# Attention over memory slots, then a three-way maxout layer, on one core: k and q of batch 0 load first, GpSimd packs k, v and ones for batches 2 to 7, and batch 0 divides its softmax by a ones product

## The chip, the cores and the metric

The kernel runs on one core of a Trainium2 chip. Its time is the device time of one execution in microseconds (us). The core has five engines with instruction queues of their own: TensorE (PE, matmuls; PEld is its weight load), VectorE (DVE), ScalarE (ACT), GpSimd (POOL) and SyncE (SP). Each engine works its queue off in order, and waits at an instruction whose inputs are not there. Loads that change the type from fp32 to bf16 are issued by GpSimd; they stand in its queue beside its other instructions.

## The reference

There are 8 batches, 8 heads, 576 positions, heads of width 64 and 32 memory slots.

```python
a = softmax(phi, axis=2)                        # (b, h, s, m)
k_m = einsum('bhsm,bhsd->bhmd', a, k)
v_m = einsum('bhsm,bhsd->bhmd', a, v)
attn = softmax(q @ k_m^T / sqrt(64), axis=-1)   # over the 32 slots
x = (attn @ v_m), heads side by side            # (4608, 512)
h = maximum(maximum(x @ w1, x @ w2), x @ w3)    # w1, w2, w3: 512 x 768
out = h @ w_out                                 # 768 x 512
```

## The kernel before

Two heads share the 128 partitions as a pair; there are NP = 4 pairs, and NC = 9 positions per partition. The kernel does not compute x. It multiplies v_m into the weights first (`fold`), so that the 32 slots of 4 heads (128 rows, two groups g) are the contraction of all large matmuls. It also uses max(a, b, c) = max(a - c, b - c) + c with w3 as c: `w_diff` takes w3 off w1 and w2 in place (for batch 0 the fold adds a second term instead, because w_diff comes later), and w3 @ w_out is made once.

The whole order of work is a list written out by hand. An item is a letter, a part and a batch (`F8@0` is part 8 of F in batch 0). The items are issued in this order, and each engine gets its share of them in this order. A "!" moves the copy out of PSUM from VectorE to ScalarE or back. The items are:

- L0, L1, L2, L3: load phi, k, v, q of a batch. H0 to H3: halves of k and v of batch 0. Y0 to Y3: w1, w2, w3, w_out. All go through GpSimd (lines 90 to 115), but for phi of batch 0, which goes through SP (line 88).
- I: the identity for transposes, made by GpSimd.
- Z: matmuls on zeros that keep TensorE at work early on (line 128). Z38 is 38 of them.
- E: exp of phi on ScalarE (line 196). B: 72 small matmuls that sum e times k, v and a constant 1 over the positions (line 209), 192 columns each; batch 1 does it in two parts, k and ones (128 columns), and v (64). kvo is the tile with k, v and ones; there are two, one for even and one for odd batches.
- N: reciprocal of the sums and the division on VectorE (lines 225 to 239). K: transpose of the result on TensorE and its copy kvt (line 254).
- Q: two VectorE transposes of q (line 269). S: scores on TensorE and their exp e2 on ScalarE (lines 291, 300).
- a, s, c, m, X: the softmax over the 32 slots on VectorE, once for each group g: a transposes 32 x 32 blocks (line 310), s sums (line 318), c takes the reciprocal (line 327), m multiplies (line 332), X transposes back into attn (line 340).
- W: w3 transposed, O: w3 @ w_out (lines 153, 161), once, with copies w3o on ScalarE. V: w_diff (line 182).
- D0, D1, D2, D4: the fold of v_m into w1 and w2, to wp (line 363); D3 into w3o, to wp3.
- F: 12 parts per batch, four matmuls each (line 389). Even parts end in a relu to h, odd parts in the max with h, which is hT (line 402).
- T: output rows, 128 at a time: six matmuls of hT with w_out (line 420), two of attn with wp3 (line 429), a copy to ot and a store on SP (line 450).

PSUM has four buffers of two banks, taken in turn by all items that use TensorE. kvo, the phi and the q tiles are there twice, so a load of batch b waits until batch b - 2 is through with its tile. A load through GpSimd also waits for the one eight places before it in the queue, since eight semaphores are used in turn.

Of the kernel before, what the change touches and what calls it, by code (L numbers as in the profile page):

```python
# [15 lines left out]
def kernel(  # L16
# [47 lines left out]
    for i in range(2):  # L64
        kvo = const.tile([P, 3, NP, NC, D], BF16, name=f"kvo{i}")
        kvos.append(kvo)
    w_sb = const.tile([P, NP, 3, DF], BF16, name="w_sb")
    w3T = const.tile([P, FT, NP, P], BF16, name="w3T")
# [6 lines left out]
    def by_pair(src, b):  # L75
        return src[b].rearrange("h s d -> (h s) d").rearrange(
            "(j p c) d -> p j (c d)", p=P, c=NC
        )

    halves = [slice(0, NP // 2), slice(NP // 2, NP)]  # L80

# [10 lines left out]
    def load_kv(b, i, h=slice(0, NP)):  # L92
        kv = loaded.setdefault(b, {})["kv"] = kvos[b % 2]
        nc.gpsimd.dma_start(  # L94
            out=kv[:, i, h].rearrange("p j c d -> p j (c d)"),
            in_=by_pair((k, v)[i], b)[:, h],
        )

# [21 lines left out]
    nc.vector.memset(warm, 0.0)  # L120
    nc.vector.memset(kvos[0][:, 2], 1.0)
    nc.vector.memset(kvos[1][:, 2], 1.0)

# [53 lines left out]
    def w_diff(n):  # L177

        c, end = n * BANK, (n + 1) * BANK
        while c < end:  # L180
# [7 lines left out]
            c = e  # L188

    st = {}  # L190

# [6 lines left out]
    def att_kv(b, part=None):  # L198
# [4 lines left out]
        cols = {None: slice(0, 3), 0: slice(0, 3, 2), 1: slice(1, 2)}[part]  # L203
        nd = {None: 3 * D, 0: 2 * D, 1: D}[part]
        for c in range(NC):
            for j in range(NP):
                for a in range(NG):
                    r = slice(HP * a, HP * (a + 1))
                    nc.tensor.matmul(  # L209
                        kvp[M * j : M * (j + 1), a, 0:nd],  # L210
                        lhsT=s["e"][r, j, c, :],
                        rhs=kv[r, cols, j, c, :],
                        start=(c == 0),
                        stop=(c == NC - 1),
                        tile_position=(HP * a, M * j),
                    )
# [59 lines left out]
    def att_score(b):  # L276
# [22 lines left out]
        for a in range(NG):  # L299
# [4 lines left out]
                scale=0.125,  # L304
            )

    def att_t(b, g):
# [176 lines left out]
    def issue(b, n, swap):  # L484

        i = int(n[1:]) if len(n) > 1 else None
        {
            "I": lambda: make_identity(nc, ident),
            "Y": lambda: load_w(i) if i < 3 else load_wo(),
            "L": lambda: load_ph(b) if i == 0 else load_q(b) if i == 3 else load_kv(b, i - 1),  # L490
            "H": lambda: load_kv(b, i % 2, halves[i // 2]),
            "E": lambda: [att_exp(b, h) for h in (halves if b == 0 else [slice(0, NP)])],
            "B": lambda: att_kv(b, i),
# [7 lines left out]
            "m": lambda: att_mul(b, i),  # L501
            "X": lambda: att_back(b, i),
            "D": lambda: fold(b, i, swap),
# [9 lines left out]
    for w in """  # L513
        H3@0 I@0 H2@0 H0@0 H1@0 E@0 Z38@0 B@0 N@0 Z3@0 K@0 L3@0 Q0@0 Q1@0 Z7@0 S@0 a0@0 Y2@0
        Y3@0 a1@0 s0@0 s1@0 c1@0 Z6@0 W0@0 W2@0 Y0@0 Y1@0 W1@0 Z10@0 O1@0 O0@0 O2@0 m1@0 D1@0!
        c0@0 m0@0 X0@0 D0@0 O3@0 L0@1 L1@1 L3@1 L2@1 X1@0 F8@0 F0@0 V0@0 F2@0 D4@0! D2@0 L0@2
        V2@0 F10@0 F6@0 F11@0 F9@0 E@1 F4@0 F3@0 F1@0 F7@0 F5@0 D3@0 B0@1 T3@0 N0@1 Q0@1 K0@1!
        T1@0 Q1@1 S@1 V1@0 E@2 L1@2 B1@1 L0@3 N1@1 a0@1 a1@1 K1@1 T2@0! s0@1 s1@1 D0@1 c0@1
        D2@1 c1@1 m0@1 D1@1! m1@1 T0@0! L2@2 X0@1 X1@1 F4@1! F5@1 L3@2 L2@3 F10@1 L1@3 F11@1
        F8@1 F0@1 F2@1 F3@1 L3@3 F6@1 F9@1 F1@1 E@3 F7@1 B@2 D3@1 N@2 Q1@2 Q0@2 T3@1 K@2! T2@1!  # L520
        S@2 a0@2 T1@1 T0@1! L0@4 D0@2 s0@2 L2@4 D1@2! a1@2 c0@2 m0@2 s1@2 c1@2 m1@2 X1@2 T4@1!
        X0@2 D3@2 L1@4 B@3 L0@5 N@3 D2@2 F6@2! Q1@3 F10@2 F2@2 F8@2 Q0@3 K@3! F3@2 F0@2 F7@2
        S@3 F1@2 F11@2 F4@2 F9@2 F5@2 E@4 D0@3 L1@5 a1@3 a0@3 D1@3! T0@2! T1@2 s0@3 D3@3 s1@3
        c1@3 m1@3 X1@3 D2@3 B@4 c0@3 E@5 T2@2! L2@5 L3@5 m0@3 X0@3 L3@4 F2@3 N@4 F0@3 F8@3
        F10@3 F1@3 F6@3 F3@3 K@4 F4@3 F7@3 F9@3 F5@3 D0@4 B@5 N@5 D1@4! F11@3 T3@2 Q0@5 K@5
        T4@3! Q1@5 S@5 L0@6 Q0@4 Q1@4 a1@5 a0@5 T1@3 s1@5 D0@5 S@4 T0@3! L0@7 s0@5 c0@5 a0@4
        c1@5 m0@5 D3@5 a1@4 m1@5 D1@5! D2@5 E@6 s1@4 X1@5 c1@4 T2@3! X0@5 s0@4 L2@7 T3@3 m1@4
        L1@7 F4@5 F0@5 F2@5 L3@7 c0@4 X1@4 m0@4 F1@5 F5@5 F3@5 X0@4 E@7 F10@5 F8@5 F9@5 D3@4
        B@7 N@7 D2@4 F11@5 F6@5 F4@4 F10@4 F8@4 Q0@7 L3@6 Q1@7 K@7 F7@5 L1@6 F0@4 Q1@6 S@7 a1@7
        L2@6 F11@4 s1@7 F5@4 a0@7 T1@5 s0@7 F6@4 c1@7 T3@5 c0@7 m0@7 F2@4 F1@4 F3@4 D1@7! D3@7  # L530
        B@6 m1@7 N@6 D2@7 T2@5! X1@7 Q0@6 K@6 F9@4 F7@4 S@6 T4@5! D0@7 a0@6 s0@6 X0@7 D0@6 a1@6
        s1@6 c1@6 m1@6 X1@6 T3@4 D3@6 D2@6 c0@6 D1@6! T0@5! T1@4 F6@7 F2@7 F0@7 m0@6 X0@6 F3@7
        F4@6 F8@6 F7@7 F9@6 F6@6 F2@6 F1@7 F5@6 F4@7 F5@7 F0@6 F7@6 F10@6 F8@7 F10@7 F9@7 F1@6
        F11@7 T2@4! F11@6 T2@7! F3@6 T1@7 T0@7! T2@6! T0@6! T3@6 T1@6 T0@4! T4@7! T3@7
    """.split():
        n, b = w.rstrip("!").split("@")
        issue(int(b), n, w.endswith("!"))
# [30 lines left out]
```

## Time and profile before

| | before |
|---|---|
| median of 5 runs | 167.4 us (166.72 to 167.59) |
| the profiled execution | 167.4 us |
| its span | 165.6 us |
| PE busy | 156.2 us (94%) |
| DVE busy | 104.6 us (63%) |
| ACT busy | 98.7 us (60%) |
| POOL busy | 28.3 us (17%) |
| moved by DMA | 31.77 MB, mean 192 GB/s |

The span runs from the first to the last instruction in the profile; the rest of the time lies around it. A matmul's end is modelled, and matmuls overlap, so the durations of single matmuls add up to more than the time they take. The chain of waits is the better guide: it lists, in order of time, the pieces of work that the end hung on. A GpSimd instruction that issues a load takes about 0.75 us there; the data arrive later.

### The profile page before, as it was taken

The page shows a single profiled execution, that of the slowest core. Times are in us where ns is not written, and L with a number is a line of the kernel's source. Part 1 is how long each engine was busy: PE and PEld are TensorE (multiplying, and loading weights), DVE is VectorE, ACT ScalarE, POOL GpSimd, SP SyncE. Part 2 cuts the span into 40 slices and gives each one's busy share as a digit, 9 for nine tenths or more (in the row PEclk, how much of TensorE's full clock was granted, in tenths as well). Part 3 has the DMA queues.
Part 4 walks back from the last instruction along what each step waited for, and adds up shares of the span by engine and source line. Part 5 has one row for each costly group of instructions (what it writes and reads, how often), then busy time and mean ns, then how long its engine had stood idle before and what let it go on. Part 6 is the DMA issues. An engine that isn't in the chain of part 4 may idle for free.

```text
span 165.6 us, 4664 instructions
## 1 busy us (share of the span) xinstructions
PE 156.2 (94%) x2006; PEld 87.6 (53%) x2024; DVE 104.6 (63%) x196; ACT 98.7 (60%) x148; POOL 28.3 (17%) x43
## 2 busy tenths in 40 slices
PE   7998799999799999999999999999999999999990
PEld 2444444674357544755674447765544678544450
DVE  5406782497686756999399798979999066610010
ACT  4200206964598458997954799993859867124320
POOL 7952110050510500710104600000000000000000
PEclk9999999999999999999999999999999999999999
DMA  5999999999999999999999999993113200024332
GB/s 151 149 204 213 205 211 225 263 208 279 311 242 257 204 243 326 259 280 213 261 238 340 233 261 235 261 205 100 69 67 123 105 32 0 35 99 183 129 150 107
DMA packets 21973, 31.77 MB, mean 192 GB/s; under 512 B 1216, under 2 KB 16576, under 8 KB 21952
## 3 DMA queue, kind: packets, MB, share of 16 engines
q0 software_dynamic: 16080, 21.43, 67.4%
q1 hardware_dynamic: 5728, 9.90, 16.9%
q8 instruction: 16, 0.26, 0.6%
q10 hardware_dynamic: 144, 0.13, 0.2%
q14 instruction: 5, 0.04, 0.1%
HBM read 39.32 MB, written 9.44 MB: 294 GB/s over the span
## 4 chain that ended last, share of the span: by engine, by line
PE 82%; DMA 10%; POOL 3%; issue 2%; ACT 0%; DVE 0%; POOLq 0%; ACTq 0%
PE acc L389 29%; PE po L420 28%; DMA wo_sb<-in_moe_w_out_dram 10%; PE po L429 8%; PE wps L363 6%; PE kvp L209 4%; PE po L161 3%; POOL kvo L94 2%; PE sc L291 2%; PE po L438 1%; PE po L461 1%; PE kvtp L254 1%; POOL qq L102 0%; POOL w_sb L108 0%; PE po L469 0%
## 5 line engine op out<-in xcount | busy, mean ns | idle before, releaser
L420 PE MATMUL po<-wo_sb,hT 128*128 128x512 bf16 x195 | 50.4, 380 | 0.8
L389 PE MATMUL acc<-attn,wp 128*128 128x288 bf16 x384 | 50.2, 286 | 0.0
L402 DVE TENSOR_TENSOR hT<-acc,h 128x576 bf16<-128x576 f32 x48 | 34.4, 752 | 15.6 <-PE acc L389 10.1
L389 PEld LDWEIGHTS <-wp 128*128 128x128 bf16 x384 | 36.8, 98 | 12.4 <-issue 1.7
L141 ACT COPY ot<-po 128x512 f32<-128x512 f32 x35 | 20.6, 592 | 30.0 <-PE po L429 24.1
L141 ACT CAST wp<-wps 128x1024 bf16<-128x1024 f32 (+1 forms) x32 | 30.4, 1003 | 4.2 <-PE wps L363 4.1
L420 PEld LDWEIGHTS <-hT 128*128 128x128 bf16 x210 | 19.2, 98 | 23.5 <-issue 3.9
L139 ACT ACTIVATE h<-acc 128x576 bf16<-128x576 f32 x46 | 27.6, 664 | 4.4 <-PE acc L389 4.0
L429 PE MATMUL po<-wp,attn 128*128 128x512 bf16 x62 | 18.4, 379 | 0.0
L128 PE MATMUL po<-warm 128*128 128x512 bf16 x62 | 16.6, 425 | 1.4 <-DVE warm L120 1.2
L332 DVE TENSOR_TENSOR t<-t,sm 128x576 bf16<-128x576 bf16 x16 | 11.8, 746 | 0.3
L128 PEld LDWEIGHTS <-warm 128*128 128x128 bf16 x64 | 6.5, 106 | 9.7 <-issue 3.3
L318 DVE TENSOR_REDUCE sm<-t 128x18 f32<-128x576 bf16 x16 | 11.5, 738 | 0.2
L269 DVE STREAM_TRANSPOSE qT<-qq 128x576 f32<-128x576 f32 x16 | 11.5, 753 | 0.0
L300 ACT ACTIVATE e<-sc 128x576 bf16<-128x576 f32 x16 | 9.6, 655 | 2.9 <-PE sc L291 2.9
L310 DVE STREAM_TRANSPOSE t<-e 128x288 f32<-128x288 f32 x16 | 7.2, 464 | 6.3 <-ACT e L300 6.2
L94 POOL DMA_DIRECT2D kvo<-in_v_dram x9 | 6.8, 755 | 23.2 <-PE wps L363 14.3
L196 ACT ACTIVATE e<-ph 128x1152 bf16<-128x1152 f32 (+1 forms) x9 | 9.7, 1072 | 1.7 <-DMA ph<-in_phi_dram 1.6
L429 PEld LDWEIGHTS <-attn 128*128 128x128 bf16 x62 | 6.1, 98 | 7.3
L90 POOL DMA_DIRECT2D ph<-in_phi_dram x7 | 5.3, 763 | 25.2 <-ACT e L196 16.8
L478 DVE COPY ot<-po 128x256 f32<-128x256 f32 x1 | 0.4, 424 | 14.2 <-PE po L469 14.2
L209 PE MATMUL kvp<-kvo,e 64*32 64x192 bf16 (+2 forms) x648 | 8.3, 235 | 1.0 <-issue 0.9
(48 smaller groups left out, 108.6 us busy)
## 6 DMA issues: line engine op xcount, KB each, us to landing
out_dram<-ot SPq DMA_DIRECT2D x35, 256.0 KB, 5.5
qq<-in_q_dram POOLq DMA_DIRECT2D x8, 576.0 KB, 18.8
ph<-in_phi_dram POOLq DMA_DIRECT2D x7, 576.0 KB, 19.3
kvo<-in_k_dram POOLq DMA_DIRECT2D x7, 576.0 KB, 18.6
kvo<-in_v_dram POOLq DMA_DIRECT2D x7, 576.0 KB, 15.8
w_sb<-in_moe_w_dram POOLq DMA_DIRECT2D x3, 768.0 KB, 19.6
wo_sb<-in_moe_w_out_dram POOLq DMA_DIRECT2D x1, 768.0 KB, 16.7
ph<-in_phi_dram SPq DMA_DIRECT2D x2, 288.0 KB, 3.0
```

The costliest lines, as they stand in the source:

```text
L94: nc.gpsimd.dma_start(out=kv[:, i, h].rearrange("p j c d -> p j (c d)"), in_=by_pair((k, v)[i], b)[:, h],)
L128: nc.tensor.matmul(po[:, 0:BANK], lhsT=warm[:, 0:P], rhs=warm, start=True, stop=True)
L139: nc.scalar.activation(out=out_, in_=in_, func=AF.Relu)
L141: nc.scalar.copy(out=out_, in_=in_)
L209: nc.tensor.matmul(kvp[M * j : M * (j + 1), a, 0:nd], lhsT=s["e"][r, j, c, :], rhs=kv[r, cols, j, c, :], start=(c == 0), stop=(c == NC - 1 ...
L269: nc.vector.transpose(out=s["qT"][:, j].rearrange("p j c r e -> p (j c r e)").bitcast(FP32), in_=loaded[b]["q"][:, j].rearrange("p j c d - ...
L318: nc.vector.tensor_reduce(out=sm, in_=s["t", g].rearrange("p n r e -> p n e r"), op=ALU.add, axis=mybir.AxisListType.X,)
L332: nc.vector.tensor_tensor(out=t, in0=t, in1=s["sm", g].unsqueeze(2).to_broadcast([P, S // HP, R, 2]), op=ALU.mult,)
L389: nc.tensor.matmul(acc[:, h, 0:SH], lhsT=wps[b][:, g, w * DF + ft * P : w * DF + (ft + 1) * P], rhs=attn[:, g, c0 : c0 + SH], start=(g == ...
L402: nc.vector.tensor_tensor(out=hT[:, ft, (b % 2) * S : (b % 2 + 1) * S].rearrange("p (h n) -> p h n", h=2), in0=a, in1=s["h1", ft], op=ALU.max,
L420: nc.tensor.matmul(po, lhsT=hT[:, fc, c0 : c0 + P], rhs=wo_sb[:, fc, :], start=(n == 0), stop=False,)
L429: nc.tensor.matmul(po, lhsT=attn[:, g, c0 : c0 + P], rhs=wp3s[b][:, g, :], start=False, stop=(g == NG - 1),)
```

## The change

The change has four parts.

1. Batch 0's loads: GpSimd first makes the identity and sets two small columns of ones, then loads k in two halves, q, w3, w_out, v in two halves, w1, w2. Before it loaded half of v, then made the identity, then k, the rest of v, q, w3, w_out, w1, w2. The k/v sums of batch 0 are split in two, as those of batch 1 already were.
2. For batches 2 to 7, GpSimd copies k and v from kvo into a tile kvr, where each position has 64 of k, 64 of v and a one. The sums then use 129 columns instead of 192.
3. For batch 0 the softmax over slots is divided by another way: a matmul with a block matrix of ones gives the sums, ScalarE takes exp(-ln) of them, and VectorE multiplies e2 by it into attn. Items M, R and X replace a, s, c, m and X there.
4. The written order is new throughout; the warm-up matmuls are 45 instead of 64.

```diff
+    kvrs = [
+        const.tile([P, NP, NC, 2 * D + 2], BF16, name=f"kvr{i}") for i in range(2)
+    ]
...
+    FULL = 2
...
+    def pack(b, i):
+        nc.gpsimd.tensor_copy(
+            out=kvrs[b % 2][:, :, :, D * i : D * (i + 1)], in_=kvos[b % 2][:, i]
+        )
...
+    blkones = const.tile([P, P], BF16, name="blkones")
+    nc.vector.memset(blkones, 0.0)
+    for i in range(P // M):
+        nc.vector.memset(blkones[M * i : M * (i + 1), M * i : M * (i + 1)], 1.0)
...
+    ln = const.tile([P, S], FP32, name="ln")
+    ONES = {(0, 0), (0, 1)}
...
-        nd = {None: 3 * D, 0: 2 * D, 1: D}[part]
+        nd = {None: 3 * D if b < FULL else 2 * D + 1, 0: 2 * D, 1: D}[part]
+        kvr = kvrs[b % 2]
...
-                        rhs=kv[r, cols, j, c, :],
+                        rhs=kv[r, cols, j, c, :]
+                        if b < FULL
+                        else kvr[r, j, c, 0:nd],
...
+    def ones_sum(b, g):
+        s = st[b]
+        e2 = s["e2"]
+        sm = acc_pool.tile([P, 2, BANK], FP32, name="sm", tag="acc")
+        for h in range(2):
+            nc.tensor.matmul(
+                sm[:, h, 0:SH],
+                lhsT=blkones,
+                rhs=e2[:, g, h * SH : (h + 1) * SH],
+                start=True,
+                stop=True,
+            )
+        s["sm", g] = sm
+
+    def ones_rec(b, g):
+        s = st[b]
+        sm = s["sm", g]
+        nc.scalar.activation(
+            out=ln.rearrange("p (h n) -> p h n", h=2),
+            in_=sm[:, :, 0:SH],
+            func=AF.Ln,
+        )
+        r = work.tile([P, S], FP32, name="r")
+        nc.scalar.activation(out=r, in_=ln, func=AF.Exp, scale=-1.0)
+        s["r", g] = r
+
+    def ones_mul(b, g):
+        s = st[b]
+        nc.vector.tensor_tensor(
+            out=attns[b // 2][:, g, (b % 2) * S : (b % 2 + 1) * S],
+            in0=s["e2"][:, g, 0:S],
+            in1=s["r", g],
+            op=ALU.mult,
+        )
...
-            "I": lambda: make_identity(nc, ident),
+            "I": lambda: [make_identity(nc, ident)]
+            + [nc.gpsimd.memset(x[:, :, :, 2 * D : 2 * D + 1], 1.0) for x in kvrs],
...
+            "r": lambda: pack(b, i),
...
-            "X": lambda: att_back(b, i),
+            "X": lambda: (ones_mul if (b, i) in ONES else att_back)(b, i),
+            "M": lambda: ones_sum(b, i),
+            "R": lambda: ones_rec(b, i),
...
-        H3@0 I@0 H2@0 H0@0 H1@0 E@0 Z38@0 B@0 N@0 Z3@0 K@0 L3@0 Q0@0 Q1@0 Z7@0 S@0 a0@0 Y2@0
-        Y3@0 a1@0 s0@0 s1@0 c1@0 Z6@0 W0@0 W2@0 Y0@0 Y1@0 W1@0 Z10@0 O1@0 O0@0 O2@0 m1@0 D1@0!
-        c0@0 m0@0 X0@0 D0@0 O3@0 L0@1 L1@1 L3@1 L2@1 X1@0 F8@0 F0@0 V0@0 F2@0 D4@0! D2@0 L0@2
...
+        E@0 I@0 H0@0 H2@0 Z25@0 B0@0 N0@0 L3@0 Z2@0 K0@0! Y2@0 Q0@0 Q1@0 Y3@0 H1@0 Z9@0 S@0
+        Z2@0 M0@0 R0@0 W1@0 X0@0 H3@0 W0@0 W2@0 M1@0 R1@0 Y0@0 Y1@0 Z7@0 O1@0 L0@1 O0@0 O2@0
+        L1@1 X1@0 L3@1 B1@0 N1@0 O3@0 K1@0 L2@1 L2@2 D3@0 L1@2 L0@2 D1@0 D0@0! F6@0 F8@0 V0@0
+        F2@0 F10@0 F0@0! D4@0 D2@0 F4@0 V1@0 F11@0 L3@2 F7@0 F5@0 F9@0 F3@0 F1@0 E@1 B0@1 N0@1
+        Q1@1 Q0@1 T1@0 K0@1! T3@0 r1@2 S@1 B1@1 V2@0 L0@3 L1@3 a0@1 s0@1 a1@1 N1@1 r0@2 s1@1
+        T2@0! K1@1 D2@1 c0@1 m0@1 L2@3 L3@3 c1@1 L1@4 L2@4 X0@1 m1@1 D1@1! X1@1 D0@1 T0@0! F8@1
...
+        N@4 D3@3 T3@2 Q0@4 K@4 F2@3 F0@3 F4@3 L0@6 Q1@4 L1@6 F3@3 L2@6 S@4 F1@3 F5@3 a0@4 L3@6
+        F10@3 F11@3 F8@3 F9@3 F6@3 s0@4 F7@3 D1@4! D2@4! E@5 r1@5 T2@3! a1@4 D3@4 L2@7 r0@5
+        D0@4 B@5 c0@4 m0@4 N@5 s1@4 T3@3 Q0@5 E@6 K@5 Q1@5 c1@4 T4@3! S@5 m1@4 T0@3! X1@4 X0@4
```

The items of the new order that the diff names r0 and r1 are the copies of k and of v for a batch.

## The prediction

> **What bounds the kernel now.** I read first the chain of waits in order of time (columns: start us, us, what). It shows what the end hangs on.
>
> ```profile
> 6.21 16.66 DMA wo_sb<-in_moe_w_out_dram
> 22.88 0.14 issue
> 23.02 3.40 PE po L161 x15
> ...
> 30.71 0.77 PE wps L363 x32
> 31.48 4.52 PE acc L389 x36
> ...
> 36.33 0.64 PE kvp L209 x72
> ...
> 41.24 0.88 issue
> ...
> 42.80 0.30 DVE kvn L229
> ...
> 47.71 5.90 PE acc L389 x48
> ...
> 77.57 0.74 PE kvp L209 x72
> ```
>
> Up to 22.9 us the end hangs on the arrival of w_out, the seventh load in GpSimd's queue. From 23.02 us to 161.56 us it is TensorE, one matmul after another. The only gaps that stand out are 0.88 and 0.30 us in batch 1; after 47.71 us there is hardly any. So there are two ways to win: start this stretch earlier, or take matmul time out of it. Everything else can only put gaps into it.
>
> Next the timeline of GpSimd, to see when loads land. From the tenth on, each load waits for the load eight places before it; the bracket is that wait.
>
> ```profile
> 9.28 0.75 POOL L90 DMA_DIRECT2D ph<-in_phi_dram  x1 [0.67 <-DMA kvo<-in_k_dram]
> 10.72 0.74 POOL L94 DMA_DIRECT2D kvo<-in_k_dram  x1 [0.69 <-DMA kvo<-in_k_dram]
> 12.16 0.74 POOL L102 DMA_DIRECT2D qq<-in_q_dram  x1 [0.70 <-DMA kvo<-in_v_dram]
> 15.00 0.74 POOL L94 DMA_DIRECT2D kvo<-in_v_dram  x1 [2.10 <-DMA qq<-in_q_dram]
> 19.63 0.75 POOL L90 DMA_DIRECT2D ph<-in_phi_dram  x1 [3.89 <-DMA w_sb<-in_moe_w_dram]
> ```
>
> Half a k or v lands every 1.44 us, a whole q takes 2.84, a weight about 4: a stream with no holes, in issue order. Last VectorE's timeline in batch 1, and the page's row of the same operation:
>
> ```profile
> 43.01 0.83 DVE L310 STREAM_TRANSPOSE t<-e 128x288 f32<-128x288 f32 x2
> 45.17 0.39 DVE L327 RECIPROCAL sm<-sm 128x18 f32<-128x18 f32 x2
> 45.48 1.42 DVE L332 TENSOR_TENSOR t<-t,sm 128x576 bf16<-128x576 bf16 x2
> 46.81 0.83 DVE L340 STREAM_TRANSPOSE attn<-t 128x288 f32<-128x288 f32 x2
> ```
> ```profile
> L332 DVE TENSOR_TENSOR t<-t,sm 128x576 bf16<-128x576 bf16 x16 | 11.8, 746 | 0.3
> ```
>
> The softmax chain ends at 47.64 us and the first matmul that needs it starts at 47.71. In batch 1 VectorE is just in time: anything that holds it there is paid by TensorE.
>
> **What the Trainium skill says.** "SBUF — State Buffer", section "Who interferes with whom": a VectorE instruction with two SBUF inputs contends with a GpSimd instruction that reads SBUF, and the later one blocks until the first is through. Here that is L332 (t and sm both in SBUF) against the new packing; the max of L402 and the other copies have one operand in PSUM. No GpSimd instruction of the trace reads an SBUF tile beside L332, so the trace neither confirms nor denies it. "GPSIMD Engine Reference", section "Elementwise — side-by-side cycle accounting": between 1.03 and 1.8 cycles per element at 1.2 GHz, by the loop. "ScalarE: Activation LUTs", section "Table sets: the hidden batching unit": ln and exp share a set, so the new Ln loads no table; the trace has one table load, of this set.
>
> **The change, part by part** (item names as in the written order; b1 is batch 1).
>
> *Order of loads.* v of batch 0 (two halves, 2 x 1.44 = 2.88 us of the stream) moves from before q to behind w_out. So q, w3 and w_out land 2.88 us earlier; w1, w2 and all behind them keep the same bytes ahead. But GpSimd now makes the identity (0.6 us from 2.06 to 2.66) and two small memsets (about 0.1 each, as the L552 memsets) before its first load, which is issued near 2.2 instead of 1.25 us. The stream loses between 0 (phi from SP's queue fills the engines until 4 us anyhow) and 1.0 us; I take 0.5. So w3_o starts at 23.02 - 2.88 + 0.5 = 20.64.
>
> *What the start can use.* From there TensorE runs, in the new order: O x4 at 1.30 (six matmuls of 512 columns; such sixes take 1.29 in the chain) = 5.20; the v half of batch 0's k/v sums, now apart, 72 matmuls of 64 columns, about 0.85 (the same for b1: 0.18 + 0.67); a wait of 0.7 for ScalarE's copy of the last O (0.59) less the small transpose beside it; D3 0.35; D1, D0 at 0.77; a wait of 0.24 for D1's copy (0.96 on VectorE); five F at 0.49 (48 matmuls in 5.90). D4 starts at 20.64 + 5.20 + 0.85 + 0.7 + 0.35 + 1.54 + 0.24 + 2.45 = 31.97, when w2 (used at 30.6 before, so there by 31.1) has landed. Before, D4 started at 30.71: 1.26 later. In exchange two F (0.98) and D3 (0.35) are done by then: 1.33. The 2.9 us won at the door are spent on the split sums and on two copies that TensorE now waits for: -0.07.
>
> *Ones product for batch 0.* Per half, two transposes, sum, reciprocal and product leave VectorE (0.46 + 0.74 + 0.25 + 0.75 + 0.46 = 2.66, 5.3 in all) and one product stays (0.75). Added: four matmuls of 288 columns (0.5) and Ln and Exp twice on ScalarE (4 x 0.66, as L300). All fall between the scores at about 15 us and 20.6 us; ScalarE idles 6.54 us there before its first copy of w3o. Cost 0; without that cover attn of batch 0 would be 2.6 us late, and it is not needed before 29. Fewer warm-up matmuls: 0 as well, they fill waits.
>
> *Narrower k/v sums.* Batches 2 to 7 go from 192 to 129 columns. The chain has 0.74 for 192 and 0.64 for 128: 0.10 x 6 = -0.6. Ends: 0 if weight loads set the pace (72 loads span 0.9 us at either width), and -1.4 if columns do (nine rounds of eight tiles, 63 columns at 0.42 ns each, x6).
>
> *Packing.* Twelve copies of 2304 elements on GpSimd: an estimate from the page above, 2.0 to 3.5 us each; I take 2.7, 32 us in all beside 28.3 us now busy. Each waits for its load, and behind it in GpSimd's queue stand loads: behind v of b2, phi and k of b3 (issued at 34.79 and 43.8 before, now near 48). The stream still has k, phi and q of b2 to move by then, so it doesn't run dry. The copies free kvo early, which lets k and v of b4 on go out sooner.
>
> *Batch 1.* In the new order nothing makes VectorE wait before b1's first transpose (the 2.25 us wait for kvn goes), so the gaps of 0.88 and 0.30 should go: -1.18. But from the end of the scores to the first F TensorE has 5.3 us of work (B1 0.74, K 0.1, T 1.72 twice, three D 1.0), and VectorE needs 0.75 for the exp and 5.4 for its items (0.83 + 1.40 + 0.39 + 1.42 + 0.83 + 0.29 + 0.19): a wait of 0.85.
>
> Sum without contention: -0.07 - 0.6 - 1.18 + 0.85 = -1.0. New gaps that a new order brings after 47.7 us, where there were none: I allow +0.7 (one copy late per two batches). That is 167.1 us.
>
> *Contention.* v of b2 is five loads behind w2: 31.1 + 1.6 + 4 x 2.88, and some 1.2 for output rows, gives 45 us; its packing runs 45 to 47.7. The scores of b1 end near 41.7; L332 is due 0.75 + 2.9 later, at 45.35, and its second at 46.7. Whichever comes first, one product stands behind a packing: 1.6 to 2.9 us, less if the packing is 2.0 us; I take 1.9, straight into TensorE's wait, as batch 1 has no slack. In b2 (6.6 us of TensorE work between scores and first F against 5.9 on VectorE) and b5 (6.5) half of such a hit shows: +0.3 in all. Batches 3, 4, 6, 7 have 9 us or more. +2.2 together. Bounds: 0 (no such hold) to +5 (both products hit in b1, b2, b5).
>
> The profiled execution took 167.4 us, 1.8 outside its span of 165.6; it is also the median shown, so nothing is to be shifted: 167.4 - 0.3 + 2.2 = 169.3.
>
> **Rivals.** *(a) Contention, 0.48:* the forecast, 169.3, own range 167.6 to 171. *(b) No hold, and the start comes out even, 0.24:* 167.1. For it: L332 is slow already (746 ns for 576 elements), so the shared interface may have room. *(c) The other side, faster, 0.16:* no hold, the first load loses nothing (-0.5) and the sums run at column rate (-0.8 more): 165.8. It decides from the start of w3_o: at 20.2 us or earlier with L332 still at 0.75 us, the gain stands. Against it: both copies that TensorE waits for are real. *(d) GpSimd late, 0.12:* between the last q transpose of b4, which frees the tile for q of b6, and the sums of b5, TensorE has 7.7 us of work; in that time GpSimd must do pack, load, pack. At 3.5 us a pack that is 7.75. Each microsecond above costs two there and about one each in b3 and b4: at 4.5 us, 171.5. That w_out doesn't come earlier would be a fifth; nothing speaks for it, as loads land in issue order.
>
> **How the numbers follow.** The measurement tells 0.3% (0.5 us) from no change. Faster: all of (c), a third of (b), little of (a): 0.16 + 0.08 + 0.03 = 0.27. Same: 0.14 of (b), 0.04 of (a): 0.18. Slower: the rest, 0.55. The range reaches from (c) at 165.8 to (d) at 171.6; signs are mixed, so (a)'s own range stands above.
>
> **What would show it.** w3_o starting near 20.6 us; D4 near 32; TensorE idle before the last w3o-dependent D3. Sums of batches 2 to 7 at 0.64 in the chain. Packing rows of 2.0 to 3.5 us. In b1 an L332 well over 0.75 us, or an idle before it ended by GpSimd, and TensorE waiting 2 to 3 us before its first L389 row of b1. If L332 stays at 0.75 us beside a running packing, (a) falls. If packings wait on one another with TensorE idle before the sums, it was (d).

## The result and the profile after

The changed kernel takes 168.34 us (median of 22 runs, 167.6 to 169.58), the kernel before 167.24 us (43 runs, 166.23 to 167.96). The ratio is 1.0071, with a 95% interval of 1.0056 to 1.0086: slower by 1.1 us between the medians. The profiled execution of the changed kernel is the slowest of the 22, 169.58 us with a span of 167.8 us; so its stages are read one by one below, and its end is not compared with the median. The ratios in this document leave out executions more than 1.5% above the fastest of their kernel: five of the twelve of the kernel packed in pieces and three of the six of the one whose packings nobody reads.

| | before | after |
|---|---|---|
| PE busy | 156.2 us | 154.6 us |
| DVE busy | 104.6 us | 106.9 us |
| POOL busy | 28.3 us | 53.7 us |
| first matmul of w3 @ w_out | 23.02 us | 21.09 us |
| accumulation of batch 1 in the chain | 47.71 us | 49.58 us |
| accumulation of batch 2 in the chain | 66.21 us | 67.81 us |

The gain at the door (the earlier start of w3 @ w_out, called w3_o below), 1.93 us, is gone by batch 1. The chain of waits of the changed kernel (start us, us, what) shows where. Line numbers have moved: L332 is now L385 (the product of the softmax), L389 is L442 (accumulation), L363 is L416 (fold), L209 is L225 (k/v sums), L340 is L393 (transpose back into attn); L104 is the packing.

```profile
8.70 23.81 DMA w_sb<-in_moe_w_dram
...
32.55 0.84 PE wps L416 x32
33.40 0.60 PE acc L442 x4
...
45.67 0.76 DVE t L385
46.95 2.07 DVE t L385
49.58 5.79 PE acc L442 x46
...
62.99 2.02 DVE t L385
65.43 0.76 DVE sm L371
66.52 0.76 DVE t L385
67.81 2.14 PE acc L442 x16
70.29 0.65 PE kvp L225 x70
```

Before, this stretch was TensorE with two small gaps. Now VectorE's softmax stands in it in batches 1 and 2, and one product in each batch takes 2.0 us instead of 0.75. The k/v sums are at 0.65 us, down from 0.74 (in batch 2 at 0.73, down from 0.87). TensorE's own timeline shows what it waits for in batch 1 (the bracket is the wait, and what ended it): two of the 48 matmuls need only the first half of attn, the others wait for the second half.

```profile
48.03 0.41 PE L442 MATMUL acc<-attn,wp 128*128 128x288 bf16 x2
49.58 2.61 PE L442 MATMUL acc<-attn,wp 128*128 128x288 bf16 x20 [1.14 <-DVE attn L393]
```

VectorE's timeline in batch 1:

```profile
45.67 0.76 DVE L385 TENSOR_TENSOR t<-t,sm 128x576 bf16<-128x576 bf16 x1
46.35 0.26 DVE L380 RECIPROCAL sm<-sm 128x18 f32<-128x18 f32 x1
46.52 0.42 DVE L393 STREAM_TRANSPOSE attn<-t 128x288 f32<-128x288 f32 x1
46.87 2.14 DVE L385 TENSOR_TENSOR t<-t,sm 128x576 bf16<-128x576 bf16 x1
```

and GpSimd's at the same time:

```profile
46.01 2.39 POOL L104 COPY kvr<-kvo 128x2304 bf16<-128x2304 bf16 x1 [12.23 <-DMA kvo<-in_v_dram]
...
62.29 2.11 POOL L104 COPY kvr<-kvo 128x2304 bf16<-128x2304 bf16 x1 [0.73 <-DMA kvo<-in_v_dram]
```

The product that starts at 46.87 ends at 49.01. The packing that runs then ends at 48.40, 0.61 us earlier. The same in batch 2: the product ends at 65.01, the packing at 64.40. A product alone takes 0.70 to 0.76 us, so nearly all of it ran when the packing was through. The other way round there is a trace of it too: the packing at 46.01 starts in the middle of a product, takes 2.39 us where the others take 2.11 or 2.12, and ends 1.97 us after that product. The reciprocal and the transpose at 46.35 and 46.52 lie inside the same packing, and are not longer than elsewhere. The page's groups put it together (busy us, mean ns of one):

```profile
L104 POOL COPY kvr<-kvo 128x2304 bf16<-128x2304 bf16 x12 | 25.6, 2137 | 33.4 <-DMA kvo<-in_v_dram 18.8
L385 DVE TENSOR_TENSOR t<-t,sm 128x576 bf16<-128x576 bf16 x14 | 13.4, 969 | 0.2
```

The mean of the product goes from 746 to 969 ns. Fourteen products at 746 would be 10.4 us, so VectorE was held for about 3 us. Only the part of it that falls in batches 1 and 2 stands in the chain.

### The profile page after: what moved, and what is told of

The parts are those of the page before. It is cut to its first block, busy times and chain, and to the rows that moved or that the text cites. A ratio compares the mean times of both kernels' runs of the same rounds, so it can differ in the third digit from the quotient of the medians.

```text
span 167.8 us, 4810 instructions
## 1 busy us (share of the span) xinstructions
PE 154.6 (92%) x2063; PEld 86.0 (51%) x2081; DVE 106.9 (64%) x195; ACT 101.5 (61%) x151; POOL 53.7 (32%) x57
## 2 busy tenths in 40 slices
DMA packets 21974, 31.77 MB, mean 189 GB/s; under 512 B 1216, under 2 KB 16576, under 8 KB 21952
## 4 chain that ended last, share of the span: by engine, by line
PE 69%; DMA 18%; DVE 8%; ACT 2%; issue 1%; POOL 0%; POOLq 0%; ACTq 0%
PE acc L442 27%; PE po L473 24%; DMA w_sb<-in_moe_w_dram 14%; PE po L482 7%; DMA kvo<-in_k_dram 4%; PE wps L416 4%; DVE t L385 3%; PE kvp L225 3%; DVE sm L371 2%; PE po L491 1%; PE sc L309 1%; DVE t L363 1%; PE po L514 1%; DVE attn L393 1%; PE kvtp L272 1%
## 5 line engine op out<-in xcount | busy, mean ns | idle before, releaser
L442 PE MATMUL acc<-attn,wp 128*128 128x288 bf16 x384 | 50.0, 286 | 2.9 <-DVE attn L393 2.2
L442 PEld LDWEIGHTS <-wp 128*128 128x128 bf16 x384 | 36.6, 98 | 15.6 <-issue 2.7
L104 POOL COPY kvr<-kvo 128x2304 bf16<-128x2304 bf16 x12 | 25.6, 2137 | 33.4 <-DMA kvo<-in_v_dram 18.8
L152 ACT ACTIVATE h<-acc 128x576 bf16<-128x576 f32 x47 | 28.6, 656 | 12.2 <-PE acc L442 12.1
L154 ACT CAST wp<-wps 128x1024 bf16<-128x1024 f32 (+1 forms) x30 | 28.5, 1008 | 3.4 <-PE wps L416 3.4
L141 PE MATMUL po<-warm 128*128 128x512 bf16 x43 | 13.0, 456 | 1.4 <-DVE warm L129 1.2
L385 DVE TENSOR_TENSOR t<-t,sm 128x576 bf16<-128x576 bf16 x14 | 13.4, 969 | 0.2
L287 DVE STREAM_TRANSPOSE qT<-qq 128x576 f32<-128x576 f32 x16 | 12.0, 763 | 1.4 <-DMA qq<-in_q_dram 1.4
L371 DVE TENSOR_REDUCE sm<-t 128x18 f32<-128x576 bf16 x14 | 10.3, 746 | 0.3
L111 POOL DMA_DIRECT2D qq<-in_q_dram x8 | 6.0, 755 | 9.9 <-DMA w_sb<-in_moe_w_dram 7.1
L416 PE MATMUL wps<-w_sb,kvt 64*32 64x512 bf16 (+1 forms) x200 | 8.4, 372 | 0.7 <-DVE kvt L158 0.5
L141 PEld LDWEIGHTS <-warm 128*128 128x128 bf16 x45 | 4.8, 113 | 7.8 <-issue 3.8
```

Source lines behind the costliest of these rows:

```text
L104: nc.gpsimd.tensor_copy(out=kvrs[b % 2][:, :, :, D * i : D * (i + 1)], in_=kvos[b % 2][:, i])
L141: nc.tensor.matmul(po[:, 0:BANK], lhsT=warm[:, 0:P], rhs=warm, start=True, stop=True)
L152: nc.scalar.activation(out=out_, in_=in_, func=AF.Relu)
L154: nc.scalar.copy(out=out_, in_=in_)
L287: nc.vector.transpose(out=s["qT"][:, j].rearrange("p j c r e -> p (j c r e)").bitcast(FP32), in_=loaded[b]["q"][:, j].rearrange("p j c d - ...
L371: nc.vector.tensor_reduce(out=sm, in_=s["t", g].rearrange("p n r e -> p n e r"), op=ALU.add, axis=mybir.AxisListType.X,)
```

## The experiments

Two theories. **A, the hold**: the change loses because products wait out packings, and without that it would be even or a little faster. **B, order and loads**: the new order or the packing as such (GpSimd's queue, late copies) costs the time, and the long products fill idle time. Ratios are to the kernel before in the same set of runs.

**Loads first.** The identity and the memsets behind the first loads instead of ahead of them.

```diff
-        E@0 I@0 H0@0 H2@0 Z25@0 B0@0 N0@0 L3@0 Z2@0 K0@0! ...
+        E@0 H0@0 H2@0 Z25@0 B0@0 N0@0 L3@0 I@0 Z2@0 K0@0! ...
```

> The changed kernel with GpSimd's first three loads ahead of the identity and the two small memsets. If the late first load is what pushed w_out and w2 back: w3_o starts 0.5 to 0.9 us earlier (near 20.3 us), D4 likewise, and the time falls by as much, to 167.6. If the stream only starts when phi's transfer is through: no change, 168.3.

Measured: 1.0065 (1.0042 to 1.0088), the same as the changed kernel. w3_o started at 20.21 us, but in the eleven other profiled executions in which batch 0's loads stood as in the changed kernel (those of the runs below among them) it started anywhere from 19.75 to 21.90 us. One start says little; the order of the first GpSimd instructions is not what the time hangs on. The products of batches 1 and 2 took up to 1.82 and 1.53 us here.

**Packing in four pieces.** Each packing as four copies of 576 elements.

```diff
-        nc.gpsimd.tensor_copy(
-            out=kvrs[b % 2][:, :, :, D * i : D * (i + 1)], in_=kvos[b % 2][:, i]
-        )
+        for j in range(NP):
+            nc.gpsimd.tensor_copy(
+                out=kvrs[b % 2][:, j, :, D * i : D * (i + 1)], in_=kvos[b % 2][:, i, j]
+            )
```

> The changed kernel with each packing in four pieces of 576 elements, one per pair. Theory A: a product waits for one piece only, so none takes more than about 1.4 us (0.75 and a piece of 0.55 to 0.6), or, if GpSimd keeps the interface from piece to piece, as long as before (2.1 us); in the first case 167.2 to 167.7 us. Theory B: no change, 168.3 us. The pieces cost GpSimd some 0.1 us each more, which nobody waits for.

Measured: 1.0039 (1.0004 to 1.0075). The products let in between two pieces take 1.07 us at most in batches 1 and 2 of the profiled execution (1.21 us in batch 3), and a row of four pieces 3.0 us beside products, 2.5 us else. That fits the hold. Whether the kernel gains by it is open: the profile is that of the fastest of twelve runs (166.07 to 169.81 us), and the median of all twelve, 168.26 us, is 1.0% above the kernel before.

**Packings in the old order.** The kernel before, in its own order, with packings and narrow sums. Where the packings stand in the list is my choice.

```diff
-        F8@1 F0@1 F2@1 F3@1 L3@3 F6@1 ...
+        F8@1 F0@1 F2@1 F3@1 L3@3 r0@2 r1@2 F6@1 ...
...
-        X0@2 D3@2 L1@4 B@3 L0@5 ...
+        X0@2 D3@2 L1@4 r0@3 r1@3 B@3 L0@5 ...
```

> The kernel before with the twelve packings and the narrow sums alone put into its own order; start, softmax of batch 0 and the rest of the order as before. Theory A: products that meet a packing take 1.5 to 2.9 us; sums 0.64 instead of 0.74. The net depends on which products meet one: 167 to 168.5 us, slower if a product of batch 1 or 2 is met. Theory B: faster than before by the sums' 0.6 us, 166.6.

Measured: 1.0411 (1.0383 to 1.044). Its chain has both faults:

```profile
46.29 2.11 POOL kvr L104
48.40 2.78 issue
51.19 2.12 POOL kvr L104
53.35 0.80 PE kvp L219 x67
...
79.58 3.61 DVE t L344
```

The sums of batch 2 wait for the packings in front of them, the second of which waits in its turn for its load, and products (L344 here) of 1.6 to 3.6 us stand in the chain of batches 2, 3 and later. So this order with packings and narrow sums is 6.8 us slower than without; the changed kernel's order spares it the first fault and most of the second. One number here is not explained: the product of 3.6 us starts 0.82 us before the packing that it ends behind (80.40 to 82.55 us), and alone it would have been through before that. GpSimd was issuing loads of q in those 0.82 us; other products beside such an issue take 0.75 or 0.76 us, as always.

**No packing.** A first form of this put the loads of k and v of a batch two further on ahead of the sums that read the same buffer, so the sums took the later batch's data and waited for it.

> The changed kernel without the twelve packings on GpSimd: the sums of all batches read kvo at 192 columns again; the start, the ones product and the written order stay. Theory A (packing and softmax product exclude each other): all L385 products at 0.75 us, no wait of TensorE before the first acc matmuls of batches 1 and 2; the packings' loss goes and six times 0.10 us come back, so 166.9 to 167.6 us. Theory B (the later start and the new order cost the time, the packings are harmless): the time stays at 168.3 or rises to 168.9 by the wider sums.

It took 196.39 us, a ratio of 1.1812, and says nothing about packing. The second form has the loads behind the sums:

```diff
-    FULL = 2
+    FULL = 8
...
-        ... r1@2 S@1 B1@1 ... r0@2 s1@1 ... L1@4 L2@4 X0@1 ... B@2 D3@1 ...
+        ... S@1 B1@1 ... s1@1 ... X0@1 ... B@2 L1@4 L2@4 D3@1 ...
```

> The changed kernel with its order of work, but without the twelve packings: the sums of all batches read k, v and ones in place, at the old width of 577 columns in three pieces, and the loads of k and v of a batch two further on stand behind the sums that read the buffer. Theory A (the hold: the normalising product of VectorE waits out a packing of GpSimd): all products take 0.75 us, the first accumulation of batch 1 starts 1.4 us earlier than in the changed kernel (near 48.2 us), that of batch 2 another 1.0 us earlier, the sums go back to 0.74 us (+0.55 in all), so the time is 1.1 - 1.4 - 1.0 + 0.55 = about -0.75 us against the kernel before, a ratio of 0.9955. Theory B (the new order and the loads are what costs, the hold only fills idle time): the time stays at +1.1 + 0.55 = +1.6 us, a ratio of 1.010.

Measured: 1.0003 (0.9982 to 1.0025), against 0.9955 by A and 1.010 by B. B falls as far as the order goes: the new order with the old sums, and the loads behind them, costs nothing that can be measured. A's direction stands, its size doesn't: the gain of 0.75 us over the kernel before isn't there. I had taken the hold (1.4 and 1.0 us) from the first profile, which is that of the slowest execution. All products take 0.69 to 0.76 us:

```profile
L385 DVE TENSOR_TENSOR t<-t,sm 128x576 bf16<-128x576 bf16 x14 | 10.2, 742 | 0.2
```

**Packings that nobody reads**, put back into that kernel in their old places:

```diff
-        ... B@2 L1@4 L2@4 D3@1 ...
+        ... r1@2 ... r0@2 ... B@2 L1@4 L2@4 D3@1 ...
```

> The kernel without packings of the same call (sums at the old width, loads of k and v behind the sums) with the twelve packings put back in their places, though nobody reads their output: the two differ by GpSimd's copies alone. Theory A (the hold): products of 2 us again in batches 1 and 2, and 2.4 us more than without the packings, a ratio near 1.010. Theory B: within 0.4 us of the kernel without packings.

Measured: 1.0196 (1.0155 to 1.0237), twice the excess that A gave; the median of all six runs, 171.1 us, is even 2.8% above the kernel before. The profiled execution, the fastest of six (169.26 to 174.41 us), has one product of 2.38 us in batch 2, and from D4 to the accumulation of batch 2 it takes 1.6 us more than without packings, about what its two held products are too long (1.62 and 0.10 us). Another 1.2 us lies in a later start of w3_o (21.40 against 20.18 us), before any packing runs. Why the other five executions took up to 5 us longer is not in this profile. That stays open, so this run agrees with A in its profile, not in its size. In this form packings stand behind loads that wait for sums, so they fall where the sums let them.

**Packings held apart, first try.** A tiny copy on GpSimd that reads a product's output stands ahead of a packing, so that the packing starts when that product is done.

```diff
+    gate_t = const.tile([P, 2], BF16, name="gate_t")
+
+    def gate(b, g):
+        nc.gpsimd.tensor_copy(out=gate_t, in_=st[b]["t", g][:, 0, 0, :])
...
-        ... T3@0 r1@2 S@1 ... N1@1 r0@2 s1@1 ... L1@4 L2@4 X0@1 m1@1 D1@1! ...
+        ... T3@0 S@1 ... N1@1 s1@1 ... X0@1 m1@1 g1@1 r1@2 r0@2 L1@4 L2@4 D1@1! ...
...
-        ... T2@1! r1@3 E@3 ... m0@2 r0@4 ...
+        ... T2@1! E@3 ... m0@2 g0@2 r1@3 r0@4 ...
```

> The changed kernel with all its packings, but held apart from the products of batches 1 and 2: both packings for batch 2 wait for the second product of batch 1 (a copy of two elements of its output on GpSimd stands ahead of them), and that of v for batch 3 waits for the first product of batch 2 in the same way. Theory A (the hold): the products of batches 1 and 2 take 0.75 us, 1.4 us and 1.0 us are gained, and the time is 1.1 - 2.4 = about -1.3 us against the kernel before, a ratio of 0.992. Theory B (order and loads cost, not the hold): no change from the changed kernel, 1.007. Theory C (GpSimd then comes late with the packed copies): the sums of batch 2 wait for GpSimd, which would stand in the chain at 51 to 54 us, and the time is at or above 1.007.

Measured: 1.0107 (1.0074 to 1.014). Batch 1 came out as A says (products 0.76 and 0.71 us), batch 2 did not. GpSimd, then VectorE in batch 2:

```profile
61.83 0.20 POOL L111 COPY gate_t<-t 128x2 bf16<-128x2 bf16 x1
61.95 2.12 POOL L104 COPY kvr<-kvo 128x2304 bf16<-128x2304 bf16 x1
```
```profile
62.53 2.16 DVE L390 TENSOR_TENSOR t<-t,sm 128x576 bf16<-128x576 bf16 x1
```

I had let the packing of batch 3 go after the first product of batch 2. Held until 61.95 us by a load, it fell on the second: 61.95 + 2.12 = 64.07, and the product ends at 64.69. The hold had only been moved. In batch 4 a product of 1.64 us stands in the chain as well, and in batch 5 one of 1.11.

**Held apart in all batches.** The packing of v for batch 3 waits for the second product of batch 2, that of k for batch 6 for the second of batch 5:

```diff
-        ... m0@2 g0@2 r1@3 r0@4 D2@2 L2@5 a1@2 ... m1@2 D1@2! ...
+        ... m0@2 D2@2 a1@2 ... m1@2 g1@2 r1@3 r0@4 L2@5 D1@2! ...
...
-        ... X0@4 r0@6 a0@5 ... m1@5 F10@4 r1@6 ...
+        ... X0@4 a0@5 ... m1@5 g1@5 r0@6 F10@4 r1@6 ...
```

> The changed kernel with its packings held apart from the products in every batch where a trace showed the two together: both packings for batch 2 wait for the second product of batch 1, that of v for batch 3 and the one behind it wait for the second product of batch 2 (in the run before it waited for the first and so fell on the second), and that of k for batch 6 waits for the second product of batch 5. Theory A (the hold alone makes the change slower): products near 0.75 us, from D4 of batch 0 to the first accumulation of batch 1 some 15.6 us (17.0 in the changed kernel), from there to the first one of batch 2 some 17.4 us (18.2), and a time like that of the kernel without packings less 0.3 to 0.5 us for the narrower sums: ratio 0.998. Theory B (it is packing as such that costs, on GpSimd's queue or by late copies): ratio 1.007 or more, with GpSimd in the chain ahead of the sums of batch 2 or 3.

> The changed kernel itself, beside the two others on one chip. Its ratio should be 1.007 again. If the hold depends on where a packing happens to fall, the products of batches 1 and 2 have other times than in the first profile (2.14 and 2.02 us for the longest), and the stretch from D4 of batch 0 to the first accumulation of batch 2 is longer or shorter than the 35.3 us of that profile by as much.

Measured side by side: held apart 0.9999 (0.9979 to 1.0018), the changed kernel itself 1.0104 (1.0063 to 1.0145); 166.76 against 168.78 us, with the same twelve packings and the same sums in both. Products of the changed kernel in this set:

```profile
44.89 2.53 DVE L385 TENSOR_TENSOR t<-t,sm 128x576 bf16<-128x576 bf16 x1
...
62.55 1.65 DVE L385 TENSOR_TENSOR t<-t,sm 128x576 bf16<-128x576 bf16 x1
```

VectorE and GpSimd of the kernel held apart:

```profile
45.44 0.76 DVE L390 TENSOR_TENSOR t<-t,sm 128x576 bf16<-128x576 bf16 x1
...
46.63 0.72 DVE L390 TENSOR_TENSOR t<-t,sm 128x576 bf16<-128x576 bf16 x1
...
63.73 0.76 DVE L390 TENSOR_TENSOR t<-t,sm 128x576 bf16<-128x576 bf16 x1
```
```profile
47.41 0.18 POOL L111 COPY gate_t<-t 128x2 bf16<-128x2 bf16 x1 [3.09 <-DVE t L390]
47.53 4.15 POOL L104 COPY kvr<-kvo 128x2304 bf16<-128x2304 bf16 x2
...
64.55 0.19 POOL L111 COPY gate_t<-t 128x2 bf16<-128x2 bf16 x1 [2.43 <-DVE t L390]
64.67 2.11 POOL L104 COPY kvr<-kvo 128x2304 bf16<-128x2304 bf16 x1
```

and its chain, which is TensorE's again from the fold to the accumulation of batch 1 and into batch 2:

```profile
45.28 0.84 PE wps L421 x24
46.12 1.40 PE po L478 x6
47.52 0.43 PE po L487 x2
47.95 5.88 PE acc L447 x48
...
63.49 1.29 PE po L478 x6
64.79 0.43 PE po L487 x2
65.22 1.96 PE acc L447 x16
67.18 0.34 PE wps L421 x8
67.52 0.65 PE kvp L230 x70
```

Later GpSimd stands in its chain, ahead of the sums of batch 6; TensorE waits 0.17 us there. Theory A gave 0.998; the interval allows it and also no gain at all.

Now the profiled executions of this order can be laid side by side (us). The chain's pieces start with the first matmul of an accumulation in some of them and with the third in others, so all are counted here to the third, the first that needs the second half of attn. "End" is the end of the last matmul, the last column the four products of batches 1 and 2:

| kernel | w3_o starts | D4 to batch 1 | on to batch 2 | on to the end | products |
|---|---|---|---|---|---|
| changed, first profile | 21.09 | 17.02 | 18.50 | 96.00 | 0.76, 2.14, 2.02, 0.76 |
| changed, again | 20.66 | 17.36 | 18.13 | 95.99 | 2.53, 0.71, 1.65, 0.76 |
| loads first | 20.21 | 16.65 | 18.02 | 96.00 | 1.82, 0.71, 1.53, 0.76 |
| held apart, first try | 19.75 | 15.71 | 18.91 | 96.61 | 0.76, 0.71, 1.02, 2.16 |
| held apart | 21.19 | 15.72 | 17.26 | 96.33 | 0.76, 0.72, 0.76, 0.76 |
| no packing, wide sums | 20.18 | 15.72 | 17.39 | 96.52 | 0.76, 0.71, 0.76, 0.76 |

From D4 to batch 2 the long products cost 2.5, 2.5, 1.7 and 1.6 us over the kernel held apart, in the order of the first four rows. That is nearly all by which they are too long. Against 0.76 us, the held products of batch 1 in the first three rows are 1.4, 1.8 and 1.1 us too long and cost 1.3, 1.6 and 0.9; those of batch 2 in the first four are 1.3, 0.9, 0.8 and 1.7 us too long and cost 1.2, 0.9, 0.8 and 1.7. Neither batch has slack to speak of. Which product is hit and for how long differs from one execution of the same kernel to the next: the first profile has batch 1's second product hit, the second its first. The narrow sums are worth 0.13 + 0.19 = 0.3 us between the last two rows; the two ratios, 0.9999 and 1.0003, come from different sets and are too close to confirm it.

**The ones product undone.** Batch 0 divides on VectorE again, in the same places of the list.

```diff
-    ONES = {(0, 0), (0, 1)}
+    ONES = set()
...
-        Z2@0 M0@0 R0@0 W1@0 X0@0 H3@0 W0@0 W2@0 M1@0 R1@0 Y0@0 ...
+        Z2@0 a0@0 s0@0 c0@0 m0@0 W1@0 X0@0 H3@0 W0@0 W2@0 a1@0 s1@0 c1@0 m1@0 Y0@0 ...
```

> The changed kernel with one part undone: batch 0 is normalised on VectorE again (transpose, sum, reciprocal, product, transpose back) in the places where the ones product and its logarithm stood. My forecast counted the ones product at nothing, with D4 of batch 0 waiting for weights at 32 us either way: the time is within 0.3 us of the changed kernel, ratio 1.005 to 1.009. Rival: VectorE, which then has 2 x 2.6 us in place of 2 x 1 us before 30 us, comes late with the differences of the weights or the first accumulation of batch 0, and the time is 1 us above the changed kernel, a ratio of 1.013.

Measured: 1.0119 (1.0084 to 1.0154), near the rival's 1.013, but not to be told from the changed kernel's own 1.0104, which is from another set. The rival's place for a loss is not there: in its profile D4 starts 11.20 us after w3_o, in the changed kernel 11.46 and 11.18 us, and VectorE is through with batch 0 at 22.3 us, long before the first accumulation. In the start the ones product neither costs nor saves anything; whether it does so elsewhere by some tenths of a per cent is left open.

**The packed layout written by the loads.** No packing at all: the loads of batches 2 to 7 go straight into kvr, in pieces of 128 bytes. They stand behind the sums, as in the kernel without packing (not shown here).

```diff
+        if b >= FULL:
+            src = by_pair((k, v)[i], b).rearrange("p j (c d) -> p j c d", c=NC)
+            for j in range(NP):
+                nc.gpsimd.dma_start(
+                    out=kvrs[b % 2][:, j, :, D * i : D * (i + 1)], in_=src[:, j]
+                )
+            return
```

> The changed kernel with its narrow sums, but nothing to pack: the loads of k and v of batches 2 to 7 write the packed layout themselves, in pieces of 128 bytes, each load as four transfers; they stand behind the sums that read the buffer. Theory A: no hold on the products, sums at 0.65 us, ratio 0.998. Rival: pieces of 128 bytes instead of 1152 make the loads several times longer, the sums of some batch wait for k or v, and the time is 1.01 or more.

Measured: 1.0698 (1.0661 to 1.0735); the rival holds. No product is held, and up to batch 2 it keeps pace with the kernel held apart (15.72 and 17.26 us). The 10.4 us by which it falls behind that kernel come later, where it waits for loads. Its page has

```profile
DMA packets 71702, 31.78 MB, mean 180 GB/s; under 512 B 57088, under 2 KB 66304, under 8 KB 71680
...
q0 software_dynamic: 65808, 21.43, 111.8%
```

71,702 packets for the same bytes as 21,974 in the changed kernel, and 111.8% of the engines' span where that has 67.0%. Its chain hangs on phi and q, which queue behind:

```profile
44.85 12.71 DMA ph<-in_phi_dram
...
58.85 12.97 DMA qq<-in_q_dram
```

So the copy on GpSimd is the cheaper of these two ways to this layout.

**The hold by itself.** After the last output row of the changed kernel, VectorE sets off a packing, spends 0.47 us on a transpose and runs one operation; the time of the whole is not to be compared.

```diff
+            if how == "read":
+                V.memset(kvos[0][:, 0, 0, 0, 0:2], 1.0)
+                pack(0, 0)
+            if how == "write":
+                V.memset(kvrs[0][:, 0, 0, 0:2], 1.0)
+                nc.gpsimd.memset(kvrs[0][:, :, :, 0:D], 1.0)
+            V.transpose(out=py, in_=px)
+            op()
```

> The changed kernel, and after its last output row a row of probes that add nothing to its output, so that its time is longer and is not to be compared. In each probe VectorE sets off a packing on GpSimd (2304 elements, 2.11 us), spends 0.45 us on a transpose, and then runs one operation of 576 elements; each operation is also run once with GpSimd at rest. The operations: the product of the kernel (two inputs in SBUF), a max of two bf16 tiles in SBUF, a max of a PSUM tile with an SBUF tile, a sum, a copy and a max with a constant in bf16, a copy in fp32; the product and the two-input max also beside a GpSimd instruction that only writes. Theory A (what the Trainium skill states in 'SBUF - State Buffer', 'Who interferes with whom': the second SBUF input goes through the interface that GpSimd reads by): the product and the two-input max run only after the packing ends, about 1.5 us late, the max with PSUM and the sum are not touched, and nothing is touched by a GpSimd that only writes; the bf16 and fp32 copies are held as well if they run in a mode that takes both ports[...], and not if they don't. Theory B (any two-engine traffic in SBUF slows both): all operations with SBUF inputs are stretched by a similar factor, the sum among them.

Measured, GpSimd and then VectorE (L224 is the product, L252 the max of two SBUF tiles, L230 that of PSUM with SBUF, L237 the sum, L246 the max with a constant, L249 the fp32 copy):

```profile
166.63 2.11 POOL L104 COPY kvr<-kvo 128x2304 bf16<-128x2304 bf16 x1 [53.47 <-DVE kvo L258]
...
186.87 2.02 POOL L262 MEMSET kvr<- 128x2304 bf16 x1 [0.40 <-DVE kvr L261]
```
```profile
165.76 0.71 DVE L224 TENSOR_TENSOR w_sb<-w_sb 128x576 bf16<-128x576 bf16 x1
...
166.80 2.54 DVE L224 TENSOR_TENSOR w_sb<-w_sb 128x576 bf16<-128x576 bf16 x1
...
173.94 0.71 DVE L230 TENSOR_TENSOR w_sb<-pp,w_sb 128x576 bf16<-128x576 f32 x1
...
176.24 0.71 DVE L237 TENSOR_REDUCE w_sb<-w_sb 128x18 f32<-128x576 bf16 x1
...
181.53 2.03 DVE L246 TENSOR_SCALAR w_sb<-w_sb 128x576 bf16<-128x576 bf16 x1
...
187.11 0.71 DVE L224 TENSOR_TENSOR w_sb<-w_sb 128x576 bf16<-128x576 bf16 x1
```

| operation, 576 elements | alone | beside a packing | beside a GpSimd memset |
|---|---|---|---|
| product, two SBUF inputs | 0.71 us | 2.54 us | 0.71 us |
| max, two SBUF inputs | 0.41 | 2.17 | 0.41 |
| max, PSUM and SBUF | 0.71 | 0.71 | |
| sum | (see below) | 0.70, 0.71 | |
| max with a constant, bf16 | 0.26 | 2.03 | |
| copy, fp32 | 0.41 | 2.17 | |

The product ends at 169.34, the packing at 168.74, 0.6 us between them, as in the kernel. Each held operation ends about 0.1 us less than its own time after the packing: the product (0.71 alone) 0.61 us after it, the two-input max and the fp32 copy (0.41) 0.31, the max with a constant (0.26) 0.16. So they wait and then run at their own pace; none is stretched. Theory A holds line by line, and B (all are stretched alike) falls with the sum and with the memset.

Two operations have no run alone in the probe, because the packing of the probe before was still going. The sum at 174.97 us, meant to be alone, lies inside the packing that starts at 173.70; its control is in the changed kernel, where sums take 0.71 to 0.74 us inside a packing and 0.73 to 0.75 outside. The bf16 copy took 2.03 us beside a packing, and 1.00 us in the run meant to be alone, which began at 177.26 us; both end 0.16 us after the packing that they met.

## Why the prediction was right or wrong

The direction and the likeliest case, (a), were right; the size was too large by the first measurement. Forecast 169.3 us, or +1.9 us; measured +1.1 us between medians of 22 and 43 runs. In the later set of six runs the changed kernel is 1.7 us above the kernel before (1.0104, 1.0063 to 1.0145), which can't be told from the forecast.

*Order of loads.* w3_o was to start at 20.64 us. The twelve profiled executions with this order of loads, or with the loads first, lie between 19.75 and 21.90 us, with the middle at 20.95. Near the forecast, though the first load is issued at 1.50 us and not near 2.2. The old order has a spread too: 23.02 us in the trace before, 21.92 in the old order with packings. So the gain at the door is nearer 1 to 2 us than the 2.4 that I took from a single trace.

*What the start can use.* D4 at 31.97, which is 11.33 us after w3_o. Measured 31.84 (11.18 after) and 32.55 (11.46, of which 0.28 is a wait for w2). Right in sum: the gain at the door is spent by D4. Its two waits are luck: I had 0.7 us for ScalarE's copy ahead of D3 and 0.24 for D1's copy; the traces show 0.3 us ahead of D3, for VectorE's copy kvt, and 0.7 us for D1's copy.

*Ones product: 0.* In the start, shown by the kernel without it.

*Narrower sums: -0.6.* In the chain they went from 0.74 to 0.65 us, 0.54 for six. What reaches the end is 0.3 us between two single profiles. Right within its bounds: the sums got shorter, so the bound of 0 falls, and the rate of -1.4 was not reached.

*Packing 2.0 to 3.5 us, taken 2.7.* Measured 2.11 us. The Trainium skill, "GPSIMD Engine Reference", section "Elementwise — side-by-side cycle accounting", gives 1.03 to 1.8 cycles per element at 1.2 GHz; 2.11 us for 2304 elements is 1.10 of them. I took the middle where the low end was right.

*Batch 1.* The old gaps of 0.88 and 0.30 us were to go and a wait of 0.85 us to come. Held apart, TensorE waits 0.17 and 0.55 us there for VectorE. Right in size; the waits stand ahead of the transpose and the fold, not ahead of the first F.

*Sum without contention: 167.1.* The kernel held apart is this case: 0.9999 of 167.4, so 167.4. It is 0.3 us above the forecast, inside the interval of 0.3 us. In part this is luck. The sum holds +0.7 us for new gaps after batch 1, and the trace shows one, of 0.17 us; against that D4 starts 0.4 us later there than forecast, and the narrow sums give 0.3 us less.

*Contention: +2.2 (1.9 in batch 1, 0.3 in batches 2 and 5).* This is the mis-sized term. The mechanism is as stated in the Trainium skill, "SBUF — State Buffer", section "Who interferes with whom": a VectorE instruction with two SBUF inputs and a GpSimd instruction that reads SBUF exclude each other; the traces and the probe agree, with 0.71 us against 2.54. But the cost is what separates the changed kernel from the one held apart: 1.05% beside it, 0.72% if the first measurement's ratio is set against the same 0.9999, so 1.2 to 1.75 us. In batch 1 the profiles show 1.3 and 1.6 us, and 0.9 in the kernel with the loads first, where I took 1.9: the packing takes 2.11 us and not 2.7, so a product behind it is held less. In batch 2 they show 1.2, 0.9 and 0.8 us, where I let half of a hit through: a hit passes whole. In batch 5 of the changed kernel there is no hit; one in batch 4 (1.25 us at 98.41 us in the first profile) isn't in the chain. Two errors in opposite directions, then: too much in batch 1, too little in batch 2. That single executions come to 2.5 us, around the forecast, is chance of where the packings land.

*Rivals.* (b), no hold, and (c), faster, fall with the products of 2 us. (c) would not have come without the hold either: the narrower sums gave 0.3 us and not 1.4, and the kernel held apart is even, not 1.6 us faster. (d), GpSimd late, doesn't happen in the changed kernel: its packings wait for loads, and no packing stands in the chain. It is real all the same, as the old order with packings shows. Its price was added up loosely: the forecast has 171.5 us in one place and 171.6 in another, and by its own terms some 4 us on top of 167.1 are 171.1. The forecast also names L332 alone as a product of two SBUF inputs; the difference of the weights (L182) is another, and meets no packing in these traces. Of the signs listed, the wait of TensorE ahead of the first accumulation of batch 1 was put at 2 to 3 us and is 1.14 us in the first profile. The idle ahead of D3 came, for another copy than I said. All others were as written.

## What to carry to other kernels

Before work that reads SBUF is given to GpSimd, list the VectorE operations that have two SBUF inputs, or that copy or take a max with a constant from SBUF to SBUF, and see which of them stand in the chain; here each that met the new work waited until it ended. A place in the list does not keep two engines apart, since GpSimd starts when its load lands: a dependency does, and here a two-element copy that reads the product's output brought back all of the loss. Then ask whether what the work buys (0.3 us here, by two single profiles) is worth even that, for the kernel held apart is no faster than the one before that can be measured.

## What the runs showed of the hardware

- The hold is whole, not a slowdown: in all profiles the product ends 0.60 to 0.63 us after the packing, wherever in the packing it began. Operations with one input in PSUM (0.75 us), sums (0.71 to 0.74), transposes and reciprocals inside a packing keep their times.
- I had looked at the product alone. Copies from SBUF (fp32, 0.41 to 2.17 us) and a max with a constant (0.26 to 2.03 us) are held too, though they have one input.
- A GpSimd memset of the same 2304 elements, 2.02 us long, holds neither the product nor the two-input max.
- A packing is held in its turn by a product that is running: 2.39 instead of 2.11 us.
- With loads in pieces of 128 bytes, 71,702 packets in place of 21,974 for the same bytes take the queue from 67.0% to 111.8% of the DMA engines' span, and the kernel is 11.6 us slower than the one before.
- When the first loads land differs between executions: with the same loads of batch 0, w3_o starts anywhere from 19.75 to 21.90 us.
